# Two small softmax steps of the first two chunks on GpSimd instead of VectorE, in an attention + MoE + MoE kernel

## The chip, the cores and the metric

The kernel runs on one core of a Trainium2 chip. Its engines are TensorE (PE in the profile; PEld is its loading of weights), VectorE (DVE), ScalarE (ACT), GpSimd (POOL) and SyncE (SP, which here issues most DMAs). They run side by side and wait for each other through semaphores; each works through its own instructions in the order in which the program put them there. The metric is the device time of one execution in microseconds (us): lower is better. Before the change the median of 3 runs is 609.37 us (606.86 to 609.39).

## The reference

Three stages follow each other, on 4 batches x 576 positions = 2304 tokens of width 512:

```
scores = scale * q @ k^T, with block-causal mask (blocks of 64)      # 4 batches, 8 heads, 64 wide
scores = scores - max(scores);  attn = exp(scores)
attn   = attn / (sum(attn) + 1e-9);  x = attn @ v                    # -> x: 2304 x 512
h = max(x @ w1, x @ w2, x @ w3);  x = h @ w_out                      # first MoE, d_ff 768
skip_score = x @ w_skip; tokens with skip_score > 0 go to their best of 8 experts:
out = x + gate * relu(x @ w1[e]) @ w2[e];  the other tokens pass through
```

The softmax row steps of interest are the maximum, its scaling, the exponential with its sum, the addition of 1e-9, the reciprocal, and the multiplication by it.

## The kernel before

The tokens are cut into 6 chunks of 384. For each chunk the attention makes x (held as a high and a low part), and then the first MoE runs over the whole chunk. The attention of chunk c+1 is laid beside the MoE of chunk c, so that chunk 0's attention stands alone at the start and chunk 1's runs beside chunk 0's MoE. The second MoE follows at the end, from about 500 us on.

A unit of attention is one tile of up to 128 query rows, for one pair of heads. Chunk 0 has 12 units (3 tiles x 4 pairs), chunk 1 has 16 (per pair a tile over 512 keys, one of 64 rows over 576 keys, one of 64 rows over 64 keys, one over 192 keys). The 64-row tiles have both heads stacked, so their row statistics are one column; the others have two columns, one for each head. The steps of a unit, with the names by which rows show them:

- PE: scores `sc` (L611, and the mask L618), into one of 2 slots of PSUM
- DVE: negated row maxima `nm<-sc` (L628, L631; with two parts also L639), then the scaling of `nm` by 0.125 (L645)
- ACT: exponentials `p<-sc,nm` (L656), one for each head, which also leave the row sums in `su`; the score slot is free after these. Where the number of keys is no multiple of 128, GpSimd clears the tail of `p` (L653)
- DVE: `r<-su`, the sums plus 1e-9 (L667; with two parts L664), then the reciprocal (L671)
- ACT or DVE: `p` times `r` (L677 on ACT, L679 on DVE)
- PE: transposes `tp` (L691); ACT or DVE copies them to `pT` (L696); PE multiplies by v, `pv` (L710); ACT and DVE write the two parts of `x` (L720, L718)

In the first 122 us the weights of the first MoE also come in, as 64-bit words: 24 pieces (18 of w1, w2, w3, 6 of w_out), each decoded by ACT (L503, L528) and DVE (L511, L513, L515, L517, L532). A w_out piece also takes PE: four transposes `pswt` (L538) and four products `psw` (L547). The MoE of a chunk has 18 groups of 12 matmuls `ps_h` (L736), then six groups of 18 `ps_y` (L787), which need all 24 pieces in chunk 0.

The order on every engine comes from a planner that runs when the program is built (`Plan.order`). `build` gives it every step as a task: the engine (or a choice of engines), an assumed duration, a due time, the tasks that it depends on, and the buffers that it takes. The planner goes through the work once, takes on each engine the ready task with the earliest due time, and the program is written out in that order. Some durations and choices: a task that depends on one of another engine is taken as ready 0.13 to 0.20 us after that one's end; the multiplication by `r` may go to ACT or DVE, except in chunk 1, where it is ACT's; the copies of the transposes may go to DVE from chunk 2 on. A changed engine of one task thus changes the whole plan behind it.

The scaling and the addition are the tasks of L224 and L231; their instructions are in `s_max_scale` (L643) and `s_sum` (L659).

Of the kernel before, what the change touches and what calls it, by code (L numbers as in the profile page):

```python
# [13 lines left out]
ALU = mybir.AluOpType  # L14
# [3 lines left out]
B, H, S, D = 4, 8, 576, 64  # L18
# [138 lines left out]
def build(S, E, groups, units):  # L157
# [14 lines left out]
    for u in units:  # L172
        c = u[1]
# [9 lines left out]
    for i, (c, b, qlo, qhi, tiles, hp) in enumerate(groups):  # L183
        at = when[first_of[i]] - 12
# [10 lines left out]
    su = []  # L195
# [8 lines left out]
    for ks in su:  # L204
        at = when[ks[0]]
        dur, acq, deps = 0.0, [], [start]
        for k in ks:
            i, c, hp, q0, nq, nk, col, first = units[k]
            dur += nk * 4 / 2400 + 0.05
            acq += ["sc"] * (2 if nk > 512 and nq == P else 1)  # L210
            deps.append(kq[i])
        sc = S.add("PE", dur, at, lambda ks=ks: [E.sc(k) for k in ks], deps, acq, mode="R")
        tps = []
        for n, k in enumerate(ks):
            i, c, hp, q0, nq, nk, col, first = units[k]
            at = when[k]
            nkt = (nk + P - 1) // P
            sets, parts = (1, 2 if nk > 512 else 1) if nq == 64 else (2, 2 if nk > 512 else 1)
            w = nk // parts
            one = dve_time(w * 2 if sets == 2 else w * parts)  # L220
            mx = S.add("DVE", one * (parts if sets == 2 else 1), at - 2, lambda k=k: E.mx(k), [sc])
            if parts == 2:
                mx = S.add("DVE", 0.07, at - 2.5, lambda k=k: E.m2(k), [mx])
            mx = S.add("DVE", 0.07, at - 2.5, lambda k=k: E.ms(k), [mx])  # L224
            exs = []
            for j in range(sets):
                exs.append(S.add("ACT", parts * (0.24 + 0.83e-3 * w), at - 2 + 0.1 * j, lambda k=k, j=j: E.ex(k, j),
                                 [mx] + exs, ["p"] if j == 0 else []))
            for _ in range(2 if nk > 512 and nq == P else 1):
                later("sc", sc, *exs)  # L230
            rs = S.add("DVE", 0.07, at - 3, lambda k=k: E.ra(k), exs)  # L231
            rs = S.add("DVE", 0.08, at - 3, lambda k=k: E.rs(k), [rs])
            nms = []
            for j in range(sets):
                nm = S.add(dict(ACT=0.19 + 0.83e-3 * nk, **(dict(DVE=0.13 + 0.52e-3 * nk) if c != 1 else {})), 0, at - 2.5 + 0.1 * j, None, [rs])
                nm.emit = lambda k=k, j=j, nm=nm: E.nm(k, j, nm.on)
                nms.append(nm)
            todo = sets * nkt
            evs = []
            for m in range(0, todo, 4):  # L240
                z = min(4, todo - m)
                tp = S.add("PE", 0.107 * z, at - 1, lambda k=k, m=m: E.tp(k, m),
                           nms + [ident] + ([tp0] if m else []),
                           ["tp"] + (["pT"] if m == 0 else []), mode="T")
                ev = S.add(dict(ACT=act_time(128 * z), **(dict(DVE=dve_time(128 * z)) if c > 1 else {})), 0, at - 5, None, [tp])
                ev.emit = lambda k=k, m=m, ev=ev: E.ev(k, m, ev.on)
                later("tp", tp, ev)
                later("p", exs[0], tp)
                if m == 0:
                    tp0 = tp  # L250
                evs.append(ev)
            last_pv[k] = (tp0, evs, nkt)
        deps, dur, acq = [], 0.0, []
        for k in ks:
            i, c, hp, q0, nq, nk, col, first = units[k]
            deps += last_pv[k][1] + [vv[i]]
            dur += last_pv[k][2] * (0.213 if nq == P else 0.107)
            acq.append("tp")
        c = units[ks[0]][1]
        if c not in x_first:  # L260
            acq.append("x")
        pv = S.add("PE", dur, when[ks[0]] - 0.5, lambda ks=ks: [E.pv(k) for k in ks], deps, acq, mode="C")
        x_first.setdefault(c, pv)
        if pv is not x_first[c]:
            pv.deps.append(x_first[c])
        for k in ks:
            i, c, hp, q0, nq, nk, col, first = units[k]
            xh = S.add("ACT", act_time(nq), when[k] - 4, lambda k=k: E.xh(k), [pv])
            xl = S.add("DVE", dve_time(nq), when[k] - 4, lambda k=k: E.xl(k), [xh])
            later("tp", pv, xl)  # L270
            later("pT", last_pv[k][0], pv)
            all_x[c] += [xh, xl]
            sc_of.setdefault(units[k][0], []).append(sc)
            pv_of.setdefault(units[k][0], []).append(pv)
# [37 lines left out]
    for c in range(NCH):  # L312
# [3 lines left out]
        for f in range(NF):  # L316
            for i in range(3):
                at = base + (3 * f + i) * 2.1
# [126 lines left out]
def _moe1_phase(tc, nc, const, small, g):  # L445
# [12 lines left out]
    with ExitStack() as st_y:  # L458
# [183 lines left out]

        def s_max_scale(k):  # L643
            nm = ud[k]["nm"][:, 0:ud[k]["sets"]]
            nc.vector.tensor_scalar(nm, nm, 0.125, None, op0=ALU.mult)  # L645

        def s_exp(k, j):
            nk, u = units[k][5], ud[k]
# [10 lines left out]
        def s_sum(k):  # L659
# [4 lines left out]
                nc.vector.scalar_tensor_tensor(r[:, 0:sets], su[:, 0, 0:sets], 1e-9, su[:, 1, 0:sets],  # L664
                                               op0=ALU.add, op1=ALU.add)
            else:
                nc.vector.tensor_scalar(r[:, 0:sets], su[:, 0, 0:sets], 1e-9, None, op0=ALU.add)  # L667

        def s_recip(k):
            r = ud[k]["r"][:, 0:ud[k]["sets"]]  # L670
# [929 lines left out]
```

## Time and profile before

| what | us |
|---|---|
| median of 3 runs (lowest, highest) | 609.37 (606.86, 609.39) |
| the profiled execution | 609.76 |
| its span, first to last instruction | 607.1 |
| PE busy | 582.6 (96%) |
| DVE busy | 349.8 (58%) |
| ACT busy | 316.7 (52%) |
| POOL busy | 43.3 (7%) |

The span is what the trace shows; 2.66 us of the profiled execution lie outside it. Busy shares are means over stages that have different limits, so they are read by stretches: the stretches below were cut where PE first runs a matmul of the first MoE (41.33 us), where the last long run of `ps_h` of chunk 0 ends (94.1 us; the first piece of w_out is turned 0.9 us later), and where `ps_y` of chunk 0 starts (122.18 us). A row of a timeline has the start, the length, the engine, the source line, the operation with its tiles and shape, and in brackets the idle time of that engine before it and what ended that.

### The profile page before, as it was taken

The page shows a single profiled execution, that of the slowest core. Times are in us where ns is not written, and L with a number is a line of the kernel's source. Part 1 is how long each engine was busy: PE and PEld are TensorE (multiplying, and loading weights), DVE is VectorE, ACT ScalarE, POOL GpSimd, SP SyncE. Part 2 cuts the span into 40 slices and gives each one's busy share as a digit, 9 for nine tenths or more (in the row PEclk, how much of TensorE's full clock was granted, in tenths as well). Part 3 has the DMA queues.
Part 4 walks back from the last instruction along what each step waited for, and adds up shares of the span by engine and source line. Part 5 has one row for each costly group of instructions (what it writes and reads, how often), then busy time and mean ns, then how long its engine had stood idle before and what let it go on. Part 6 is the DMA issues. An engine that isn't in the chain of part 4 may idle for free. (4 is left out here: it accounts for less than half of the span.)

```text
span 607.1 us, 11847 instructions
## 1 busy us (share of the span) xinstructions
PE 582.6 (96%) x4338; PEld 495.5 (82%) x4338; DVE 349.8 (58%) x1022; ACT 316.7 (52%) x825; POOL 43.3 (7%) x101
## 2 busy tenths in 40 slices
PE   6889999899999999999999999999999999899994
PEld 3568798699888998988978889988899997688732
DVE  4899999925555346555366562565533675258600
ACT  4998869942757424545245444375641541158420
POOL 1000000002000010000200000200001011311101
PEclk9999999999999999999999999999999999899998
DMA  6564754421110220103211223100016752799980
GB/s 184 159 203 140 217 159 142 138 92 60 51 30 23 72 90 24 41 21 94 75 44 48 62 77 110 44 22 23 1 37 213 250 179 49 238 363 366 343 288 23
DMA packets 61096, 72.74 MB, mean 120 GB/s; under 512 B 7571, under 2 KB 40597, under 8 KB 61024
## 3 DMA queue, kind: packets, MB, share of 16 engines
q1 hardware_dynamic: 59424, 68.88, 35.5%
q0 software_dynamic: 1600, 2.96, 1.5%
q8 instruction: 39, 0.64, 0.5%
q14 instruction: 33, 0.27, 0.1%
HBM read 61.13 MB, written 11.04 MB: 119 GB/s over the span
## 5 line engine op out<-in xcount | busy, mean ns | idle before, releaser
L736 PE MATMUL ps_h<-x,w 128*128 128x384 f32 x1296 | 244.7, 341 | 0.5 <-DVE hm L745 0.5
L736 PEld LDWEIGHTS ps_h<-x,w 128*128 128x128 f32 x1296 | 222.4, 188 | 5.5 <-issue 3.3
L656 ACT ACTIVATE p<-sc,nm 128x288 f32<-128x288 f32 (+7 forms) x168 | 85.0, 516 | 29.6 <-DVE nm L645 28.9
L696 ACT COPY pT<-tp 128x512 f32<-128x512 f32 (+2 forms) x108 | 53.3, 511 | 47.9 <-PE tp L691 46.7
L611 PE MATMUL sc<-k,q 64*64 64x288 f32 (+9 forms) x384 | 67.8, 453 | 6.4 <-DMA q<-in_kq_dram 4.7
L691 PE MATMUL tp<-cst_sb,p 128*128 128x128 f32 x432 | 65.9, 281 | 3.9 <-ACT pT L696 1.8
L787 PE MATMUL ps_y<-wo,h_h 128*128 128x256 f32 (+1 forms) x360 | 68.8, 287 | 0.0
L691 PEld LDWEIGHTS tp<-cst_sb,p 128*128 128x128 f32 x432 | 49.7, 143 | 17.7 <-issue 8.0
L710 PE MATMUL pv<-pT,vt 128*64 128x128 f32 (+1 forms) x960 | 60.4, 270 | 1.6 <-ACT pT L696 1.5
L631 DVE TENSOR_REDUCE nm<-sc 128x2 f32<-128x256 f32 (+7 forms) x64 | 51.3, 811 | 15.8 <-PE sc L618 10.3
L710 PEld LDWEIGHTS pv<-pT,vt 128*64 128x64 f32 x960 | 48.0, 138 | 13.8 <-issue 4.9
L787 PEld LDWEIGHTS ps_y<-wo,h_h 128*128 128x128 f32 x360 | 56.7, 189 | 1.2 <-issue 1.2
L787 PE MATMUL ps_y<-wo,h_l 128*128 128x256 f32 (+1 forms) x180 | 51.1, 284 | 0.0
L611 PEld LDWEIGHTS sc<-k,q 64*128 64x128 f32 (+1 forms) x384 | 29.5, 178 | 24.2 <-issue 11.3
L677 ACT ACTIVATE p<-p,r 128x576 f32<-128x576 f32 (+8 forms) x73 | 42.3, 596 | 9.0 <-DVE r L671 8.3
L745 DVE TENSOR_TENSOR hm<-ps_h,ha 128x384 f32<-128x384 f32 x36 | 20.0, 555 | 34.6 <-PE ps_h L736 33.2
L720 ACT CAST x<-pv 128x128 fp32r<-128x128 f32 (+1 forms) x80 | 20.0, 263 | 31.2 <-PE pv L710 30.8
L656 ACT ACTIVATION_READ_ACCUMULATOR p<-sc,nm 128x1 f32 x168 | 35.0, 208 | 0.0
L745 DVE TENSOR_TENSOR hm<-ps_h,hm 128x384 f32<-128x384 f32 x36 | 20.0, 555 | 25.2 <-PE ps_h L736 24.6
L787 PEld LDWEIGHTS ps_y<-wo,h_l 128*128 128x128 f32 x180 | 34.0, 189 | 0.0
L718 DVE TENSOR_TENSOR x<-pv,x 128x128 fp32r<-128x128 f32 (+1 forms) x80 | 21.1, 274 | 21.6 <-ACT x L720 20.8
L749 ACT CAST h_h<-hm 128x384 fp32r<-128x384 f32 x36 | 18.5, 515 | 28.0 <-DVE hm L745 27.9
(220 smaller groups left out, 678.8 us busy)
## 6 DMA issues: line engine op xcount, KB each, us to landing
raw<-in_m_w_dram SPq DMA_DIRECT2D x19, 1024.0 KB, 7.2
raw<-in_w_dram SPq DMA_DIRECT2D x18, 512.0 KB, 3.8
vt<-in_v_dram SPq DMA_DIRECT2D x16, 320.0 KB, 3.3
x<-y SPq DMA_DIRECT2D x18, 256.0 KB, 2.1
out_dram<-y SPq DMA_DIRECT2D x18, 256.0 KB, 2.4
xa<-in_m_w_dram SPq DMA_DIRECT2D x4, 1024.0 KB, 6.8
xb<-in_m_w_dram SPq DMA_DIRECT2D x4, 1024.0 KB, 7.8
raw<-in_w_out_dram SPq DMA_DIRECT2D x6, 512.0 KB, 3.5
```

The costliest lines, as they stand in the source:

```text
L611: nc.tensor.matmul(bank[:, 0:hi - lo], gd["q"][rows, q0:q0 + nq], gd["k"][rows, lo:hi], start=True, stop=packed or hi != nk)
L631: nc.vector.tensor_reduce(nm, first_ps[:, :, 0:w], axis=AX.X, op=ALU.max, negate=True)
L656: nc.scalar.activation(u["p"][:, j, lo:hi], src, AF.Exp, bias=u["nm"][:, j:j + 1], scale=0.125, accum_out=u["su"][:, n, j:j + 1])
L677: nc.scalar.activation(pt, pt, AF.Copy, scale=r)
L691: nc.tensor.transpose(tp[:, n, :], u["p"][:, j, t * P:(t + 1) * P], ident)
L696: copy(u["pT"][:, m:m + z], u["tp", m][:, 0:z])
L710: nc.tensor.matmul(pv[64 * j:64 * j + 64, 0:nq], vt[:, t, 64 * j:64 * j + 64], pT, start=(t == 0), stop=(t == nkt - 1))
L718: nc.vector.tensor_tensor(xl, pv, xh, op=ALU.subtract)
L720: nc.scalar.copy(xh, pv)
L736: nc.tensor.matmul(ps, a[:, d, :], x[:, d, :], start=(n == 0), stop=(n == 3 * ND - 1))
L745: nc.vector.tensor_tensor(nxt, hm_at["ps", i], hm_at[f], op=ALU.max)
L787: nc.tensor.matmul(ps, a[:, f, hs], x[:, f, lo:hi], start=(n == 0), stop=(n == 3 * NF - 1))
```

## The change

In chunks 0 and 1 the scaling of the maxima, and the addition of 1e-9 where the row sums are in one part, are GpSimd's. The maxima, the exponentials, the reciprocals and the multiplications stay where they were. That is 28 scalings (12 in chunk 0, 16 in chunk 1; 20 of two columns, 8 of one) and 24 additions (all 28 units but the four over 576 keys).

```
--- before.py
+++ after.py
@@ -221,14 +221,14 @@
             mx = S.add("DVE", one * (parts if sets == 2 else 1), at - 2, lambda k=k: E.mx(k), [sc])
             if parts == 2:
                 mx = S.add("DVE", 0.07, at - 2.5, lambda k=k: E.m2(k), [mx])
-            mx = S.add("DVE", 0.07, at - 2.5, lambda k=k: E.ms(k), [mx])
+            mx = S.add("POOL" if c < 2 else "DVE", 0.07, at - 2.5, lambda k=k: E.ms(k), [mx])
...
-            rs = S.add("DVE", 0.07, at - 3, lambda k=k: E.ra(k), exs)
+            rs = S.add("POOL" if c < 2 and parts == 1 else "DVE", 0.07, at - 3, lambda k=k: E.ra(k), exs)
             rs = S.add("DVE", 0.08, at - 3, lambda k=k: E.rs(k), [rs])
...
         def s_max_scale(k):
             nm = ud[k]["nm"][:, 0:ud[k]["sets"]]
-            nc.vector.tensor_scalar(nm, nm, 0.125, None, op0=ALU.mult)
+            eng = nc.gpsimd if units[k][1] < 2 else nc.vector
+            eng.tensor_scalar(nm, nm, 0.125, None, op0=ALU.mult)
...
             else:
-                nc.vector.tensor_scalar(r[:, 0:sets], su[:, 0, 0:sets], 1e-9, None, op0=ALU.add)
+                eng = nc.gpsimd if units[k][1] < 2 else nc.vector
+                eng.tensor_scalar(r[:, 0:sets], su[:, 0, 0:sets], 1e-9, None, op0=ALU.add)
```

The source lines behind the change move by one or two (L667 of before is L669, L671 is L673, L691 is L693, L710 is L712, L736 is L738, L787 is L789).

On DVE, the first softmaxes of chunk 0 (`nm` maxima, `r` sums, `p` exponentials), before:

```order
L631 TENSOR_REDUCE nm<-sc 128x2
L645 TENSOR_SCALAR nm<-nm 128x2
L631 TENSOR_REDUCE nm<-sc 128x2
L645 TENSOR_SCALAR nm<-nm 128x2
L667 TENSOR_SCALAR r<-su 128x2
L671 RECIPROCAL r<-r 128x2
L679 TENSOR_SCALAR p<-p,r 128x128
L631 TENSOR_REDUCE nm<-sc 128x2
L667 TENSOR_SCALAR r<-su 128x2
```

and the same place on DVE in the changed kernel:

```order
L631 TENSOR_REDUCE nm<-sc 128x2 x2
L673 RECIPROCAL r<-r 128x2
L681 TENSOR_SCALAR p<-p,r 128x128
L631 TENSOR_REDUCE nm<-sc 128x2
L673 RECIPROCAL r<-r 128x2
L681 TENSOR_SCALAR p<-p,r 128x256
L631 TENSOR_REDUCE nm<-sc 128x2
```

The rows L645 and L667 are gone from here; the reciprocal now waits for GpSimd. Until the first `ps_h` product is read, two multiplications of `p` of 128x384 have also gone from DVE (6 before, 4 now) to ACT (2 before, 4 now).

The steps taken from DVE stand on GpSimd in the changed kernel like this, from behind the constants on (numbers are those of the buffers; before, GpSimd had nothing there up to the first clearing of `p`, in chunk 1):

```order
L646 TENSOR_SCALAR nm_184<-nm_184 128x2
L669 TENSOR_SCALAR r_199<-su_187 128x2
L669 TENSOR_SCALAR r_219<-su_192 128x2
L646 TENSOR_SCALAR nm_211<-nm_211 128x2
L646 TENSOR_SCALAR nm_235<-nm_235 128x2
L669 TENSOR_SCALAR r_269<-su_239 128x2
```

Scalings and additions of neighbouring units take turns in one queue, each behind the one in front of it.

On PE, a part of the stretch in which w_out is turned (`pswt`, `psw`) beside the last units of chunk 1, before:

```order
L710 MATMUL pv<-pT,vt 64x64 x10
L691 MATMUL tp<-cst_sb,p 128x128
L547 MATMUL psw<-wr_sb,wt 128x10 x4
L710 MATMUL pv<-pT,vt 64x64 x2
L691 MATMUL tp<-cst_sb,p 128x128 x4
L538 MATMUL pswt<-cst_sb,dec 128x128 x4
L611 MATMUL sc<-k,q 64x64 x2
L710 MATMUL pv<-pT,vt 64x128 x4
L547 MATMUL psw<-wr_sb,wt 128x10 x4
```

and on PE in the changed kernel, a part of the same stretch:

```order
L738 MATMUL ps_h<-x,w_121 128x384 x12
L538 MATMUL pswt<-cst_sb,dec 128x128 x4
L693 MATMUL tp<-cst_sb,p 128x128 x5
L611 MATMUL sc<-k,q 64x64 x2
L547 MATMUL psw<-wr_sb,wt 128x10 x4
L538 MATMUL pswt<-cst_sb,dec 128x128 x4
L712 MATMUL pv<-pT,vt 64x64 x2
L712 MATMUL pv<-pT,vt 64x128 x4
L738 MATMUL ps_h<-x,w_121 128x384 x12
L547 MATMUL psw<-wr_sb,wt 128x10 x4
```

Groups of `ps_h` now stand between the steps of w_out: behind the first `pswt` there are 3 of the 18, where before there was 1. In return the two pairs of scores of chunk 2 (over 320 and 448 keys), which stood in front of `ps_y` of chunk 0, stand behind it and one `ps_h` group. From the MoE of chunk 2 on, PE's order is the same in both kernels.

## Rows read from the trace of the kernel before

**Rows 1.** Stretches: length; busy us (x instructions) of each engine; granted clock, DMA share, GB/s

```profile
4.00:16.00 12.00, 10.45 (x52) 6.30 (x52) 6.95 (x26) 6.02 (x23) 0.00 (x0) 1.00 0.77 218
16.00:41.33 25.33, 20.78 (x186) 12.54 (x184) 23.95 (x77) 24.44 (x77) 0.15 (x1) 1.00 0.55 156
41.33:94.10 52.77, 52.77 (x393) 46.30 (x392) 52.16 (x126) 41.96 (x95) 0.61 (x4) 1.00 0.60 182
94.10:122.18 28.08, 25.77 (x252) 20.46 (x249) 25.69 (x87) 25.32 (x80) 1.93 (x9) 1.00 0.46 133
122.18:500.00 377.82, 377.32 (x2985) 342.58 (x2984) 193.83 (x595) 180.36 (x497) 22.60 (x52) 1.00 0.23 72
```

**Rows 2.** Waits of PE, 16 to 41.33 us: for what; us in total, times, longest

```profile
PE tp L691 <- ACT pT L696: 1.0, 2, 0.6
PE tp L691 <- DVE x L718: 1.0, 2, 0.5
PE sc L611 <- ACT p L656: 0.9, 2, 0.7
```

**Rows 3.** Waits of PE, 94.1 to 122.18 us

```profile
PE pv L710 <- ACT pT L696: 1.0, 2, 0.8
PE tp L691 <- ACT pT L696: 0.8, 1, 0.8
```

**Rows 4.** Timeline of DVE about the small steps, 42 to 43 us

```profile
42.38 0.16 DVE L667 TENSOR_SCALAR r<-su 128x2 f32<-128x2 f32 x1
42.45 0.15 DVE L639 TENSOR_TENSOR nm<-nm 128x1 f32<-128x1 f32 x1
...
42.98 0.15 DVE L645 TENSOR_SCALAR nm<-nm 128x1 f32<-128x1 f32 x1
43.09 0.43 DVE L513 TENSOR_SCALAR dec<-dec 128x512 int32<-128x512 int32 x1
```

**Rows 5.** The scaling (L645) until 122.18 us: its durations, who waited for it

```profile
L645 DVE TENSOR_SCALAR nm<-nm x30: 131/158/170, 6.8 to 121.2; 128x2 f32<-128x2 f32 x22, 128x1 f32<-128x1 f32 x8
...
  ACT p L656: 7.4, 6
```

**Rows 6.** Timeline: maxima of a unit on DVE, its first exponential on ACT, two units

```profile
6.35 0.42 DVE L631 TENSOR_REDUCE nm<-sc 128x2 f32<-128x256 f32 x1 [4.78 <-PE sc L618]
...
7.08 0.37 ACT L656 ACTIVATE p<-sc,nm 128x128 f32<-128x128 f32 x1 [4.83 <-DVE nm L645]
...
18.25 0.40 DVE L631 TENSOR_REDUCE nm<-sc 128x2 f32<-128x256 f32 x1
...
19.88 0.37 ACT L656 ACTIVATE p<-sc,nm 128x128 f32<-128x128 f32 x1
```

**Rows 7.** Groups until 122.18 us by shape: busy us, mean ns of one

```profile
L677 ACT ACTIVATE p<-p,r 128x384 f32<-128x384 f32 x2 | 1.2, 615 | 0.0
...
L515 DVE SCALAR_TENSOR_TENSOR dec<-raw,dec 128x512 int32<-128x512 int32 x24 | 16.5, 686 | 0.0
...
L511 DVE TENSOR_SCALAR dec<-dec 128x512 f32<-128x512 f32 x24 | 10.2, 424 | 0.7 <-ACT dec L503 0.6
```

**Rows 8.** Groups on POOL in the whole span, by shape

```profile
L653 POOL MEMSET p<- 128x64 f32 x16 | 2.5, 154 | 162.5 <-PE tp L691 88.8 <-DVE hm L745 48.6 <-ACT pT L696 11.8
...
L970 POOL IOTA eidx<- 128x8 f32 x1 | 0.1, 127 | 0.0
```

**Rows 9.** Timeline: a DVE step of the decoding and a clearing on POOL, 95.2 us

```profile
95.24 0.52 DVE L511 TENSOR_SCALAR dec<-dec 128x512 f32<-128x512 f32 x1
95.28 0.20 POOL L653 MEMSET p<- 128x128 f32 x1 [12.56 <-ACT dec L503]
```

**Rows 10.** Timeline: two groups of ps_h; scores of chunk 2, their first multiplication by r

```profile
41.33 4.45 PE L736 MATMUL ps_h<-x,w 128*128 128x384 f32 x24
...
117.52 0.81 PE L611 MATMUL sc<-k,q 64*128 64x320 f32 x4
...
123.85 0.39 DVE L679 TENSOR_SCALAR p<-p,r 128x320 f32<-128x320 f32 x1
```

## The prediction, as it stood before the changed kernel ran

> **What bounds the kernel now.** I first cut the span into stretches and read the busy time of each engine in them [rows 1]. From 122.18 to 500 us PE is idle for 0.5 of 377.8 us, with DVE and ACT about half idle: there PE is the bound, and nothing that DVE or ACT save can shorten it. The change is in the stretches before. From 4 to 16 us no engine is full. From 16 to 41.33 us, with chunk 0's attention and the first decoding, PE idles 4.55 us, DVE 1.4 and ACT only 0.9: ACT is the fullest engine, DVE close behind. From 41.33 to 94.10 us PE has no idle time at all, and DVE 0.6. From 94.10 to 122.18 us PE idles 2.3 us, DVE 2.4, ACT 2.8: each waits for the others.
>
> A gain must come out of PE's idle time up to 122.18 us: 1.55 + 4.55 + 0 + 2.31 = 8.4 us [rows 1], since PE's own work stays the same. Then I asked what these idle times wait for. From 16 to 41.33 us it is the copies of the transposes on ACT, the second part of x on DVE, and exponentials that hold the score slots, about 1 us each [rows 2]; later, 1.8 of 2.3 us are copies on ACT [rows 3]. So more of it is ACT's work than DVE's, although ACT's work is itself late when DVE is.
>
> Because PE is full behind 122.18 us, and its order is the same from the MoE of chunk 2 on, what is won or lost before it should reach the end whole.
>
> **The steps that go from DVE.** 28 scalings and 24 additions leave it. One takes 131 to 170 ns by its own record [rows 5], but DVE starts the next one sooner: the addition at 42.38 is followed at 42.45, the scaling at 42.98 at 43.09 [rows 4]. So a step occupies DVE for 0.07 to 0.11 us, 0.09 in the middle, and 52 of them for 4.7 us: 2.2 us for chunk 0's 24, 2.5 us for chunk 1's 28.
>
> **The steps that come to GpSimd.** It has 0.15 us of work up to 41.33 us and 2.5 us from there to 122.18 [rows 1], so it has room. How long a two-column step lasts there no row shows. The nearest are the iota of 128x8 (127 ns) and the clearing of 128x64 (154 ns), and the longer clearing of 128x128, 0.20 us [rows 8, 9]. I take 0.2 us, as the new step also reads, and bound it by 0.1 and 0.5. With a second hand-over between engines, I take 0.4 us from the end of the maxima to the exponential.
>
> Before, that way took 0.31 us when nothing lay between (maxima end at 6.77, exponential starts at 7.08) and 1.23 us for a usual unit (18.65 to 19.88) [rows 6]. In all of 30 units until 122.18 us ACT was idle only 6 times for the scaling, and 4.8 of those 7.4 us are the first unit of all [rows 5, 6]. So 0.4 us on GpSimd costs about 0.1 us on a handful of units and nothing on the others: ACT is busy with other work, or the scaling stood in DVE's queue behind decoding steps of 0.42 or 0.69 us [rows 7], which it now passes. I set hand-overs at zero, with +0.6 us as the bound (six units by 0.1). The cover is ACT's backlog; without it, the price is that of the last rival.
>
> The new waits: a reciprocal on DVE now waits for GpSimd, and behind it in DVE's queue stand maxima and decoding steps. Before, it waited for the addition in the same queue, which waited for the same exponentials. The difference is one hand-over, some 0.1 to 0.3 us of DVE for 24 units if DVE has no backlog, so at most what the change frees; in the stretches where DVE is full it is covered.
>
> **The order that comes with it.** Up to the first group of ps_h two multiplications of 128x384 go from DVE to ACT, 0.615 us each [rows 7], 1.2 us on the engine that has only 0.9 us idle from 16 us on. Up to 41.33 us the bounds are thus a gain of 2.2 us plus these two steps (at most 0.8 us on DVE, as no such step there is longer than the 424 ns of one over 512 columns [rows 7]) if DVE decides, so 3.0, and a loss of 1.2 us if ACT does. I take a gain of 0.5, a little below the middle (0.9), since ACT is the fuller engine [rows 1].
>
> From 41.33 to 122.18 us the limits are 0 and 2.31 us. DVE's freed 2.5 us are about PE's idle time, and three groups of ps_h instead of one now stand between the steps of w_out, where PE idled; a pair of groups is 4.45 us of PE work that waits for no copy of a transpose [rows 10]. I take 1.5 us.
>
> The two pairs of scores of chunk 2 move behind ps_y. Their PE time moves with them and costs nothing, but their softmax starts later. Before, from 117.52 us to the first multiplication at 123.85 was 6.3 us, hidden under ps_y [rows 10]. Now the cover behind them is two groups of ps_h, 4.45 us. The bounds are 0 and the 1.9 us between; DVE and ACT were delayed by the last units of chunk 1 at that time and are freer behind ps_y, so I take 0.2 us.
>
> Sum: 0.5 + 1.5 - 0.2 = 1.8 us off the profiled execution's 609.76, so 608.0. The median of the runs lies 0.4 us below that execution; I forecast 607.6 for the median.
>
> **Rivals.**
>
> *All that DVE gives is PE's.* DVE decides in both stretches: 2.2 + 2.3 = 4.5 us, so 604.9. For it: DVE is full from 41.33 to 94.10 and nearly so before [rows 1]. Against it: PE has no idle time in that same stretch, and the waits name ACT more often than DVE [rows 2, 3].
>
> *Nothing arrives.* ACT's extra 1.2 us eats what chunk 0 gives, and PE's idle time around w_out stays, since its waits are for ACT's copies [rows 3]: 609.4. For it: ACT's 0.9 us of slack from 16 us on.
>
> *Slower: VectorE and GpSimd hold each other up.* At 95.24 us a decoding step lasts 0.52 us instead of its mean of 0.42, and the one clearing that GpSimd has in that time starts within it [rows 7, 9]. If a GpSimd step that reads has to wait for the decoding step it meets, the 28 scalings come late. The decoding is 24 pieces of two steps of 0.42 and three of about 0.69, 2.9 us, or 70 us of the 106 us from 16 to 122 us. A scaling thus meets it two times in three; if it had to sit out the rest of a whole piece (1.45 us in the middle), it would be late by 0.95 us. Two score slots hide half; if half the units have spare time as that at 18.65 us has, 14 x 0.48 = 6.7 us are lost, less 1.8 won: about 614. It decides from a mean delay of 0.3 us on (14 x 0.15 = 2 us). Against it: the steps of a piece seldom stand in a row on DVE, others lie between, and the effect seen is 0.1 us.
>
> The Trainium skill has this as a rule (SBUF — State Buffer, "Who interferes with whom"): a VectorE step in a two-port mode, or with two SBUF inputs against a GpSimd step that reads, shares one port pair with GpSimd, and whoever starts first holds it to the end. By that rule all five decoding steps lock out the new GpSimd steps, and the result is this rival if the lock is taken again at once; the trace agrees as far as the 0.52 us go, but it has no GpSimd step here that reads.
>
> **How the numbers follow.** Forecast 607.6 (its own range 606.0 to 609.0): 0.48. All of it, 604.9: 0.18. Nothing, 609.4: 0.22. Slower, 614: 0.12. From the low case down to about 604.6 and from the slow one up to 612 the range leaves out 0.2. A change of 0.5% (3.0 us) is about what a measurement can tell from none: faster is below 606.3, slower above 612.4. Faster: 0.17 of the low case and a seventh of the forecast, 0.24. Slower: 0.1. The same: 0.66.
>
> **What the profile will show.** Right, if: PE's first ps_h starts between 40 and 42 us and ps_y of chunk 0 between 117 and 119 (some 1.6 us of that are only the moved scores); PE's idle time between them falls below 1.5 us; the steps on GpSimd last 0.1 to 0.3 us; ACT's waits for the scaling stay few. Wrong, if GpSimd's steps last 0.5 us or more, or ACT's waits for them grow beyond some 5 us without the first unit; if PE has new gaps of over 1 us behind ps_y; or if the stretch from the MoE of chunk 2 on changes its length by over 1 us, which would be a cause that is not in this sum.

## The result, and the profile after

The changed kernel takes 612.59 us in the median of 10 runs, the kernel before 609.37: a ratio of 1.0058, 95% interval 1.0042 to 1.0074. By that ratio it is slower by 3.5 us (3.2 us between the medians), where the prediction had it faster by 1.8. The profiled execution took 612.66 us, with a span of 610.8. Three executions in all, of 951 and 1132 us (the kernel before) and 1430 us (kernel 3 below), lie far from every other and are in no ratio and no mean.

Where the time went is read from a few moments that both kernels have, and from the fact that PE does the same products up to them.

| moment (us) | before | after | difference |
|---|---|---|---|
| first `ps_h` of chunk 0 | 41.33 | 43.48 | +2.15 |
| first `ps_y` of chunk 0 | 122.18 | 120.32 | -1.86 |
| first `ps_h` of chunk 2 | 220.40 | 224.09 | +3.69 |
| end of the span | 607.1 | 610.8 | +3.7 |

In this pair of profiles nothing is won or lost from the MoE of chunk 2 on: 386.7 us in both. (Over the profiles of all kernels below, this last part takes 384.3 to 388.0 us.) The stretches of the changed kernel, cut where [rows 1] are cut and once more at chunk 2 (length; busy us and instructions of PE, PEld, DVE, ACT, POOL; granted clock, DMA share, GB/s):

```profile
4.00:16.00 12.00, 9.99 (x50) 6.11 (x52) 4.65 (x14) 7.08 (x25) 1.74 (x8) 1.00 0.78 214
16.00:43.48 27.48, 22.39 (x189) 13.29 (x187) 23.25 (x61) 24.48 (x77) 5.79 (x18) 1.00 0.50 146
43.48:94.10 50.62, 50.05 (x396) 43.11 (x394) 49.55 (x114) 43.60 (x103) 6.52 (x18) 1.00 0.62 184
94.10:120.32 26.22, 25.49 (x224) 22.28 (x223) 23.82 (x66) 20.62 (x62) 5.27 (x20) 1.00 0.49 143
120.32:224.09 103.77, 103.15 (x833) 93.36 (x830) 48.49 (x143) 47.90 (x136) 5.92 (x16) 0.98 0.19 58
```

PE's idle time between `ps_h` and `ps_y` is 0.57 + 0.73 = 1.3 us where it was 2.31 [rows 1], so the part of the forecast that counted idle time came out by 1.0 of 1.5 us. But the granted clock of the last row is below 1, and it was 1.00 before. The same view over all the work up to chunk 2, and up to the first `ps_h`, of the kernel before:

```profile
0.00:220.40 220.40, 208.00 (x1681) 175.34 (x1682) 151.67 (x449) 147.44 (x407) 9.45 (x40) 1.00 0.40 118
4.00:41.33 37.33, 31.23 (x236) 18.85 (x236) 30.89 (x102) 30.46 (x99) 0.15 (x1) 1.00 0.62 176
```

and of the changed one:

```profile
0.00:224.09 224.09, 211.06 (x1681) 178.16 (x1682) 150.34 (x401) 145.17 (x403) 27.11 (x92) 0.99 0.39 116
4.00:43.48 39.48, 32.38 (x237) 19.40 (x237) 27.90 (x74) 31.57 (x102) 7.54 (x26) 1.00 0.59 167
```

The 3.69 us are 0.63 us more idle time (12.40 to 13.03) and 3.06 us that the same 1681 products last longer (208.00 to 211.06). Of these, 1.15 us lie before the first `ps_h` (31.23 to 32.38; the 237th product there is the `ps_h` at the edge). In both kernels PE's first products last nearly twice as long as the same ones later, and in the changed kernel this slow start lasts longer. Scores over 384 keys in the kernel before:

```profile
7.94 1.65 PE L611 MATMUL sc<-k,q 64*128 64x384 f32 x4 [0.57 <-ACT p L656]
...
16.09 0.92 PE L611 MATMUL sc<-k,q 64*128 64x384 f32 x4
```

and in the changed one, with the transposes behind them (six of them last 0.88 us later on):

```profile
15.57 1.63 PE L611 MATMUL sc<-k,q 64*128 64x384 f32 x4
17.18 1.31 PE L693 MATMUL tp<-cst_sb,p 128*128 128x128 f32 x6
...
25.02 0.92 PE L611 MATMUL sc<-k,q 64*128 64x384 f32 x4
```

These two rows alone are 1.14 us. The same scores take 1.63 us in the profiles of kernels 1, 3, 9 and 14 below too, which open in the changed kernel's order, and 1.65 in that of kernel 2, which has the order of before. The granted clock of these stretches is shown as 1.00 all the same. Another 1.7 us lie in one place, where `ps_y` of chunk 0 begins:

```profile
117.10:120.50 3.40, 3.39 (x31) 2.87 (x32) 2.75 (x9) 2.25 (x7) 0.38 (x2) 1.00 0.29 75
120.50:123.90 3.40, 3.40 (x17) 3.40 (x18) 0.64 (x4) 1.38 (x6) 0.23 (x1) 0.50 0.27 76
```

From 120.5 to 123.9 us PE ran at half its clock, 1.2 GHz in place of 2.4, and got through 17 products; in a kernel with the same order that kept its clock (the first experiment) it is 32 in the same stretch. Ahead of the fall stand the small products of the last two pieces of w_out (`psw`, 10 columns) and of chunk 1's last units.

The waits of PE from 16 us to the first `ps_h`, beside [rows 2], are of the same kinds; what stands out is the time that ACT's copies come late (us in total, times, longest):

```profile
PE pv L712 <- ACT pT L698: 1.9, 3, 1.0
PE tp L693 <- DVE p L681: 0.9, 1, 0.9
PE tp L693 <- ACT p L679: 0.7, 2, 0.4
```

From 94.1 us to `ps_y`, the 1.8 us of waits for copies [rows 3] are gone; these are left:

```profile
PE sc L611 <- ACT p L657: 0.6, 1, 0.6
PE pswt L538 <- DVE dec L517: 0.2, 1, 0.2
```

The scalings on GpSimd answer to [rows 5]:

```profile
L646 POOL TENSOR_SCALAR nm<-nm x28: 213/234/888, 6.8 to 119.8; 128x2 f32<-128x2 f32 x20, 128x1 f32<-128x1 f32 x8
...
who waited for it (us, times):
  ACT p L657: 10.1, 9
```

Their median is 0.234 us, near the 0.2 that was assumed, the longest 0.888. ACT waited 10.1 us, 9 times, where it was 7.4 us, 6 times. So the steps themselves look much as foreseen, and the question is what else changed.

### The profile page after: what moved, and what is told of

Read it like the earlier page. It is cut to its first block, busy times and chain, and to the rows that moved or that the text cites. A ratio compares the mean times of both kernels' runs of the same rounds, so it can differ in the third digit from the quotient of the medians.

```text
span 610.8 us, 11846 instructions
## 1 busy us (share of the span) xinstructions
PE 585.7 (96%) x4338; PEld 500.2 (82%) x4338; DVE 348.3 (57%) x974; ACT 314.6 (51%) x821; POOL 62.3 (10%) x153
## 5 line engine op out<-in xcount | busy, mean ns | idle before, releaser
L738 PE MATMUL ps_h<-x,w 128*128 128x384 f32 x1296 | 245.2, 341 | 0.5 <-DVE hm L747 0.5
L738 PEld LDWEIGHTS ps_h<-x,w 128*128 128x128 f32 x1296 | 222.2, 188 | 6.7 <-issue 4.0
L698 ACT COPY pT<-tp 128x512 f32<-128x512 f32 (+2 forms) x102 | 50.2, 509 | 47.9 <-PE tp L693 47.2
L789 PE MATMUL ps_y<-wo,h_h 128*128 128x256 f32 (+1 forms) x360 | 70.8, 292 | 0.0
L693 PE MATMUL tp<-cst_sb,p 128*128 128x128 f32 x432 | 65.7, 281 | 3.4 <-DVE p L681 0.9
L693 PEld LDWEIGHTS tp<-cst_sb,p 128*128 128x128 f32 x432 | 50.0, 143 | 16.8 <-issue 6.7
L712 PE MATMUL pv<-pT,vt 128*64 128x128 f32 (+1 forms) x960 | 60.0, 270 | 2.7 <-ACT pT L698 2.6
L712 PEld LDWEIGHTS pv<-pT,vt 128*64 128x64 f32 x960 | 47.9, 138 | 15.2 <-ACT pT L698 6.6
L789 PEld LDWEIGHTS ps_y<-wo,h_h 128*128 128x128 f32 x360 | 58.1, 193 | 1.3 <-issue 1.2
L789 PE MATMUL ps_y<-wo,h_l 128*128 128x256 f32 (+1 forms) x180 | 51.9, 288 | 0.0
L611 PEld LDWEIGHTS sc<-k,q 64*128 64x128 f32 (+1 forms) x384 | 29.9, 180 | 24.6 <-issue 10.2
L789 PEld LDWEIGHTS ps_y<-wo,h_l 128*128 128x128 f32 x180 | 34.7, 193 | 0.0
L796 ACT COPY y<-ps_y 128x256 f32<-128x256 f32 x30 | 11.2, 373 | 45.1 <-PE ps_y L789 45.0
```

The lines of the kernel that those rows point to most:

```text
L611: nc.tensor.matmul(bank[:, 0:hi - lo], gd["q"][rows, q0:q0 + nq], gd["k"][rows, lo:hi], start=True, stop=packed or hi != nk)
L693: nc.tensor.transpose(tp[:, n, :], u["p"][:, j, t * P:(t + 1) * P], ident)
L698: copy(u["pT"][:, m:m + z], u["tp", m][:, 0:z])
L712: nc.tensor.matmul(pv[64 * j:64 * j + 64, 0:nq], vt[:, t, 64 * j:64 * j + 64], pT, start=(t == 0), stop=(t == nkt - 1))
L738: nc.tensor.matmul(ps, a[:, d, :], x[:, d, :], start=(n == 0), stop=(n == 3 * ND - 1))
L789: nc.tensor.matmul(ps, a[:, f, hs], x[:, f, lo:hi], start=(n == 0), stop=(n == 3 * NF - 1))
```

## Experiments

Theory "order": the plan behind the changed engine puts the work of all engines into another order, and that order is worse. Rival "GpSimd": its steps are late or hold VectorE up. A third came up with the rows above, "clock": PE's clock falls to half, whatever brings it about. The table has every kernel that ran: its ratio to the kernel before on the same chip, the granted clock averaged over its runs (the kernel before has 0.995), and from the one profiled execution the first `ps_h`, the first `ps_h` of chunk 2, PE's idle time up to there, and the half clock before that.

| kernel | ratio (95%) | mean clock | ps_h 0 | ps_h 2 | idle | half clock |
|---|---|---|---|---|---|---|
| before | 1 | 0.995 | 41.33 | 220.40 | 12.40 | none |
| after | 1.0058 (1.0042 to 1.0074) | 0.990 | 43.48 | 224.09 | 13.03 | 3.4 us at 120.5 |
| 1 after's order, no GpSimd | 1.0040 (1.0023 to 1.0057) | 0.993 | 43.44 | 222.50 | 12.59 | none |
| 2 before's order, GpSimd | 0.9994 (0.9981 to 1.0007) | 0.994 | 42.21 | 221.20 | 12.12 | none |
| 3 chunk 0 alone | 1.0011 (0.9993 to 1.0030) | 0.994 | 41.92 | 224.06 | 12.40 | 3.4 us at 121.8 |
| 4 chunk 1 alone | 0.9927 (0.9910 to 0.9945) | 0.996 | 41.30 | 219.55 | 10.86 | none |
| 5 order of 4, no GpSimd | 1.0001 (0.9987 to 1.0016) | 0.995 | 41.46 | 220.55 | 12.01 | none |
| 6 before's order, no steps | 0.9983 (0.9967 to 0.9999) | 0.996 | 40.90 | 219.77 | 11.77 | none |
| 7 before, assumed 0.09 | 1.0091 (1.0059 to 1.0123) | 0.987 | 40.23 | 226.81 | 13.46 | 10.2 us at 115.8 |
| 8 after, early products | 1.0055 (1.0033 to 1.0076) | 0.991 | 43.83 | 222.92 | 10.43 | 3.4 us at 23.8 |
| 9 after, filled | 1.0062 (1.0042 to 1.0082) | 0.993 | 43.68 | 223.32 | 13.17 | none |
| 10 kernel 7, filled | 1.0087 (1.0065 to 1.0109) | 0.989 | 39.71 | 225.44 | 13.20 | 6.8 us at 118.0 |
| 11 after, assumed 0.35 | 1.0001 (0.9986 to 1.0015) | 0.995 | 39.84 | 220.39 | 13.08 | none |
| 12 kernel 4 again | 0.9971 (0.9957 to 0.9985) | 0.996 | 41.09 | 219.32 | 10.85 | none |
| 13 after, multiplications at home | 1.0017 (0.9999 to 1.0036) | 0.991 | 40.62 | 223.37 | 10.78 | 6.8 us at 118.1 |
| 14 after, assumed 0.20 | 0.9999 (0.9985 to 1.0013) | 0.994 | 44.29 | 224.79 | 12.61 | 6.8 us at 103.6 |
| 15 before, assumed 0.11 | 1.0016 (0.9997 to 1.0035) | 0.993 | 44.23 | 221.75 | 13.94 | none |

A profile is one execution of many: that of kernel 14 is the slowest of its 12 (614.16 us, median 609.46), those of kernels 2 and 4 are the slowest of their 12 and 6, those of kernels 5, 9 and 10 the fastest of their 12, 6 and 6, that of kernel 7 is close to its median.

The first `ps_h` does not have the same work ahead of it everywhere: 236 or 237 products in most kernels, 230 or 231 in kernels 3, 7, 10 and 11 (some 1.2 us less), 245 in kernel 14. And over the table it does not go with the ratio (correlation 0.08): kernels 14 and 15 have it latest and are level with the kernel before, kernel 7 has it early and is the slowest. The first `ps_h` of chunk 2 goes with the ratio (0.81).

### 1 and 2: the order without GpSimd, GpSimd without the order

Kernel 1 is the changed kernel with its plan as it is, but the steps executed by VectorE:

```
-            eng = nc.gpsimd if units[k][1] < 2 else nc.vector
-            eng.tensor_scalar(nm, nm, 0.125, None, op0=ALU.mult)
+            nc.vector.tensor_scalar(nm, nm, 0.125, None, op0=ALU.mult)
```

and likewise for the addition. Kernel 2 is the reverse: the kernel before with only these lines of the change, the planner still believing in VectorE.

> The order of the changed kernel on every engine, but the scalings and additions of chunks 0 and 1 are executed by VectorE again, at the places where the plan had them on GpSimd. Theory 'order' (the loss comes from the order that the planner made on a wrong idea of GpSimd's cost): as slow as the changed kernel or slower, 612 to 615 us, first ps_h group at 43 us or later. Theory 'engine' (GpSimd's steps themselves come late, through hand-overs and VectorE's decoding steps that lock them out): the loss is gone, 608 to 610 us, first ps_h group near 41.5 us.

> The order of the kernel before on every engine, but the 28 scalings and 24 additions are executed by GpSimd. Theory 'order': no loss, 607 to 609.5 us (VectorE is freed of some 4.7 us of work), first ps_h at 41.5 us or earlier. Theory 'engine': the loss is here, 611 to 614 us, first ps_h at 43 us.

Measured: 1.0040 for the order alone, 0.9994 for GpSimd alone. The order carries most of the loss with no step on GpSimd, and the very same steps cost nothing that the runs can tell in the order of before. Kernel 1's first `ps_h` is at 43.44, the changed kernel's at 43.48. (Kernel 2's profile has it 0.88 us late, all of it by the longer slow start: PE's products ahead of it take 32.33 us in place of 31.23.) Kernel 1's profile lost no clock at `ps_y`, the same stretch as above:

```profile
120.50:123.90 3.40, 3.40 (x32) 3.33 (x30) 0.88 (x6) 2.40 (x9) 0.00 (x0) 1.00 0.29 87
```

So with one order the clock fell in one kernel's profile and not in the other's. Kernel 1's runs have a mean clock of 0.993 against 0.990 for the changed kernel; whether GpSimd has a part in that is not shown: the two ratios, 1.0040 and 1.0058, have intervals that overlap.

### 3 and 4: one chunk at a time

The changed kernel with the condition `< 2` set to `== 0` (kernel 3) or `== 1` (kernel 4), in plan and instructions, planned anew.

> The change in chunk 0 alone (12 units), planned anew. If the loss is made in the stretch of chunk 0's attention (first ps_h 2.2 us late in the changed kernel), the whole loss or most of it is here: 611 to 613 us. If it is made beside the decoding of chunk 0's MoE, 609 to 610 us. Theory 'engine' has fewer locked-out steps here than in chunk 1 (9 of 24 GpSimd steps over 0.3 us), theory 'order' makes no statement on the sign but says that the first ps_h moves with the order.

> The change in chunk 1 alone (16 units), planned anew. If chunk 0's stretch makes the loss, this is at or below the kernel before: 606.5 to 609.5 us, as the stretch from 41 us to ps_y gained in the changed kernel. If steps locked out by VectorE's decoding make it, this is the slow half: 611 to 613 us.

Chunk 0 alone is level with the kernel before (1.0011), chunk 1 alone is faster than both (605.88 us, 0.9927). The two do not add up to 1.0058: each change of the engine plans everything behind it again.

### 5 and 12: is kernel 4's gain its order, GpSimd, or the chip?

Kernel 5 has kernel 4's order, but its steps on VectorE, by the edit of kernel 1. Kernel 12 is kernel 4 once more, on another chip.

> The order of the kernel that has the change in chunk 1 alone, but its scalings and additions executed by VectorE. If the 4 us that kernel won over the kernel before come from the order, this one wins most of them too: 605.5 to 607, with ps_y of chunk 0 starting near 120. If they come from VectorE's freed 2.5 us, this one loses them: 608.5 to 610.

> The change in chunk 1 alone once more, on the chip and beside the kernel before of this call: its 605.9 (0.993 of the kernel before) rest on 6 runs of one chip, and its order with the steps on VectorE ran at 1.000 on another. If the gain is the kernel's, 0.991 to 0.995; if it was the chip's, 0.998 to 1.001.

Kernel 5 came out at 1.0001, so the order alone gains nothing. Kernel 12 at 0.9971: the gain is there on a second chip, but less than half of it (607.48 us). PE's idle time up to chunk 2 shows the size: 12.01 us in kernel 5, 10.85 and 10.86 in kernels 12 and 4. So with chunk 1 alone the step that the prediction foresaw is real, 1.1 us in the profile. The runs' 0.3 to 0.7% are 1.8 to 4.4 us; no row shows where the rest of that comes from.

### 6: no steps at all

The order of before; the 52 steps do nothing in chunks 0 and 1, and the reciprocal reads the sums.

```
-            nc.vector.tensor_scalar(nm, nm, 0.125, None, op0=ALU.mult)
+            if units[k][1] >= 2:
+                nc.vector.tensor_scalar(nm, nm, 0.125, None, op0=ALU.mult)
...
```

> The order of the kernel before, with the 28 scalings and the 24 additions of chunks 0 and 1 left out altogether (the scaling of the maximum and the 1e-9 are missing from those two chunks). This takes the whole 4.7 us from VectorE with no GpSimd step and no hand-over. If VectorE's time is worth what the prediction's low rival said, 604.9; by the prediction's own two terms 607.6; if an order that stays as it was gives nothing back, 609 to 609.8.

0.9983, or 1.0 us (0.1 to 2.0 by the interval). That is all that VectorE's 4.7 us are worth in that order, with no hand-over to pay.

### 7 and 15: another order without any change of engine

```
-            mx = S.add("DVE", 0.07, at - 2.5, lambda k=k: E.ms(k), [mx])
+            mx = S.add("DVE", 0.09 if c < 2 else 0.07, at - 2.5, lambda k=k: E.ms(k), [mx])
```

Kernel 15 has 0.11 in its place.

> The kernel before with the duration that the planner assumes for the scalings of chunks 0 and 1 set to 0.09 us in place of 0.07, still on VectorE: no instruction changes, only the order from the end of chunk 0's attention on. If any other order of this stretch may move the time by some 3 us, it need not come out at the kernel before's 609.6: outside 608.6 to 610.6. If the loss of the changed kernel needs its own order or GpSimd, this one is within 1 us of the kernel before.

> The kernel before with 0.11 us in place of 0.07 as the assumed duration of the scalings on VectorE; 0.09 ran at 1.009 of the kernel before. If a larger number makes the plan worse step by step, it is at 1.009 or more. If the orders are draws around the kernel before, it may be anywhere from 0.993 to 1.010, with its half clock before 130 us and its first ps_h telling which.

An assumed duration that is changed by 20 ns makes the kernel 0.9% slower, no less than the whole change does; changed by 40 ns it is 0.16% slower, which the interval does not tell from nothing. So the loss does not grow with the number, and a loss of this size needs neither GpSimd nor the change. In kernel 7 it is the clock, in the stretch where w_out is turned:

```profile
112.40:115.80 3.40, 2.41 (x25) 1.61 (x24) 3.37 (x13) 2.84 (x11) 0.20 (x1) 1.00 0.46 131
115.80:119.20 3.40, 3.35 (x17) 2.57 (x16) 2.85 (x10) 1.16 (x5) 0.00 (x0) 0.50 0.03 6
119.20:122.60 3.40, 2.77 (x14) 2.77 (x14) 1.25 (x9) 2.38 (x9) 0.00 (x0) 0.50 0.31 89
122.60:126.00 3.40, 3.40 (x18) 3.40 (x17) 0.05 (x1) 1.45 (x4) 0.00 (x0) 0.50 0.00 0
126.00:129.40 3.40, 3.40 (x34) 3.20 (x33) 0.42 (x2) 0.75 (x3) 0.00 (x0) 0.99 0.29 87
```

PE had 1.0 us without work, the clock went to 0.50, and each stretch then held 14 to 18 products in place of 34. Half of 10.2 us is 5.1 us; the ratio stands for 5.5. (Up to chunk 2 this profile loses 6.4 us, 5.35 of them in longer products, and it gets 2.4 back behind it.)

### 8: products in front, against the slow start

PE's slow start lasts until about 16 us before and until about 18 us after (the rows over 384 keys in the section on the result).

```
+                if k == 0:
+                    for _ in range(20):
+                        nc.tensor.matmul(ps[0:64, 1, 384:512], mask_k, mask_q, start=True, stop=True)
```

> The changed kernel with 20 products of the two mask tiles (64 x 128, bf16) in front of PE's first scores, into a part of a score tile that nobody reads; PE waits for its first queries there until 4.0 us. If PE's slow first 18 us (a pair of 64x64 bf16 products at 0.26 us in place of 0.20) are part of the loss, the first ps_h starts near 42.3 in place of 43.5 and the time falls to about 611.3. If the order alone sets the first ps_h, it stays at 43.2 to 43.6, and the time at 612.2 to 612.9.

The ratio stayed at 1.0055, so nothing was won in the runs, and the first `ps_h` at 43.83. But this profile does not rule the slow start out. The early products did shorten it: the scores over 384 keys at 15.68 us took 1.54 us in place of 1.63, the six transposes behind them 0.88 in place of 1.31, and the next transposes start at 18.51 in place of 18.95. Then, at 23.8 us, the clock fell, as it did not in the changed kernel's profile:

```profile
20.40:23.80 3.40, 1.89 (x23) 1.22 (x18) 3.25 (x12) 3.40 (x11) 0.60 (x2) 1.00 0.20 59
23.80:27.20 3.40, 3.40 (x18) 1.82 (x15) 2.04 (x8) 2.46 (x10) 0.95 (x3) 0.50 0.32 107
```

and took the lead away. How much of the late first `ps_h` the slow start makes is left open by this run. (Its idle time in the table is less because the 20 products fill idle time at the start.)

### 9 and 10: products against the half clock

```
+            if k >= 22:
+                for _ in range(2):
+                    nc.tensor.matmul(ps.rearrange("p d c -> p (d c)")[:, 0:CH], w_piece(0, 0, 0)[:, 0, :], hid[0][:, 0, :], start=True, stop=True)
             for d in range(ND):
                 nc.tensor.transpose(ps[:, d, :], c[:, d * P:(d + 1) * P], ident)
```

> The changed kernel, with two more products of 128x384 (0.19 us each at full clock) in front of the transposes of each of the last two pieces of w_out, in PE's queue; nobody reads them. They add at most 0.8 us. If the loss is PE's clock, which fell to half at 120.5 us behind the small products of these pieces, it falls there less often: no half clock between 100 and 130 us, and the time between 611 and 611.9. If the order costs the time without the clock, the time goes up by 0.4 to 0.8 us: 613.0 to 613.4.

> The same filling (two products of 128x384 ahead of each of the last three pieces of w_out) in the kernel whose planner assumed 0.09 us for the scalings on VectorE, which ran at 613.5 with 10 us of half clock from 115.8 us on and PE idle 1.7 us before ps_y. Filling costs at most 1.1 us. If the half clock is the loss, 609 to 611. If not, 613.5 to 614.6.

Kernel 9's profile (the fastest of its 6 runs) has no half clock before 500 us, and PE's busy time up to chunk 2 is 0.9 us below the changed kernel's (211.06 to 210.15) although 0.8 us of products were added. But the runs give 1.0062, no gain. Kernel 10 still fell, 6.8 us in place of 10.2, and stayed at 1.0087. So filling moves the clock a little (0.990 to 0.993, 0.987 to 0.989) and does not pay. As a test of the clock it is inconclusive for kernel 9 and a miss for kernel 10, where the fall was not prevented.

### 11 and 14: the assumed duration of the GpSimd steps

```
-mx = S.add("POOL" if c < 2 else "DVE", 0.07, ...)
+mx = S.add("POOL" if c < 2 else "DVE", 0.35 if c < 2 else 0.07, ...)
```

and the same for the addition; 0.20 in kernel 14.

> The changed kernel with 0.35 us in place of 0.07 as the duration that the planner assumes for the steps on GpSimd, near what they lasted (0.33 to 0.38 in the mean). If the loss comes from a plan that prices these steps wrongly, it goes: 608.5 to 610. If any new order of this stretch draws its loss or gain anew, nothing ties it to either kernel: it may lie from 605 to 614, and its time goes with the half clock before 130 us and with the first ps_h.

> The changed kernel with 0.20 us in place of 0.07 as the assumed duration of the steps on GpSimd; 0.35 ran at 1.000 of the kernel before, 0.07 at 1.006. If what counts is how near the assumed duration is to the 0.33 to 0.38 that they lasted, it lies between: 609.5 to 612. If every new order draws its time anew, it may come out anywhere from 605 to 614, on either side of both.

Both are level with the kernel before: 1.0001 and 0.9999. The loss is gone with either number. With 0.35 the first `ps_h` starts at 39.84 us, and no clock was lost:

```profile
0.00:220.39 220.39, 207.31 (x1682) 175.49 (x1682) 147.93 (x398) 147.78 (x406) 30.70 (x92) 1.00 0.39 118
```

That fits a price that had been wrong, but 0.20 fits as well as 0.35, and its profile has the first `ps_h` later than any other (44.29, with 245 products ahead of it). I take it that two more orders were drawn and both were better, not that a right price gives a good order.

### 13: the multiplications back on their engines

In the changed kernel the planner may put each multiplication by `r` on ACT or DVE. Here chunk 0's are tied to the engines they had before:

```
...
+                if c == 0:
+                    home = "DVE" if (k, j) in ON_DVE else "ACT"
+                    both = {home: both[home]}
...
```

> The changed kernel, with each multiplication by r of chunk 0 tied to the engine that it had in the kernel before (14 on VectorE, 10 on ScalarE), so that none moves to ScalarE; the rest is planned anew. If the 2.15 us lost at the first ps_h are the multiplications that moved to ScalarE, it starts between 41 and 42 us, and the time falls to 609.5 to 611. If the rest of the new order loses them, it stays at 43 to 44 and the time at 612 to 613.

The first `ps_h` starts at 40.62 us, 2.9 us earlier, and the ratio falls from 1.0058 to 1.0017. So the plan in which the multiplications stay at home has no late first `ps_h`; but that plan differs in more than the multiplications. What happens to the first of them, one of 256 columns, is seen on ACT. First the changed kernel (start, length, operation; idle time before and what ended it, in brackets):

```profile
10.80 0.51 ACT L679 ACTIVATE p<-p,r 128x256 f32<-128x256 f32 x1
...
11.87 0.59 ACT L657 ACTIVATE p<-sc,nm 128x384 f32<-128x384 f32 x1
...
13.25 0.61 ACT L657 ACTIVATE p<-sc,nm 128x384 f32<-128x384 f32 x1
...
14.76 1.23 ACT L679 ACTIVATE p<-p,r 128x384 f32<-128x384 f32 x3
18.31 0.86 ACT L698 COPY pT<-tp 128x512 f32<-128x512 f32 x2 [2.32 <-PE tp L693]
```

then DVE beside it:

```profile
14.28 0.17 DVE L673 RECIPROCAL r<-r 128x2 f32<-128x2 f32 x1 [1.98 <-POOL r L669]
14.56 0.42 DVE L681 TENSOR_SCALAR p<-p,r 128x384 f32<-128x384 f32 x1
```

and kernel 13, the same unit on ACT, then on DVE:

```profile
11.09 0.58 ACT L664 ACTIVATE p<-sc,nm 128x384 f32<-128x384 f32 x1 [0.31 <-POOL nm L653]
...
11.99 0.59 ACT L664 ACTIVATE p<-sc,nm 128x384 f32<-128x384 f32 x1
...
16.09 0.58 ACT L705 COPY pT<-tp 128x512 f32<-128x512 f32 x1 [0.69 <-PE tp L700]
```

```profile
13.00 0.17 DVE L680 RECIPROCAL r<-r 128x2 f32<-128x2 f32 x1 [0.58 <-POOL r L676]
13.20 0.75 DVE L688 TENSOR_SCALAR p<-p,r 128x384 f32<-128x384 f32 x2
```

In the changed kernel the multiplication of 256 columns stands on ACT ahead of the exponentials of the next unit, which start at 11.87 in place of 11.09; then the exponentials of two units take turns, and the second one over these 384 keys starts at 13.25 in place of 11.99. The reciprocal is 1.28 us later, DVE stands idle for 1.98 us, its multiplication has its twin on ACT, in a group of three that ends at 15.99, and ACT then waits 2.32 us for PE. DVE's "<-POOL" names the last link of that chain: the addition of 0.2 us on GpSimd waited for the exponentials.

That the multiplications moved is not enough for the loss, though. Kernel 11 also has 4 of 384 columns on ACT, and one of 256 columns, at 11.34 us, ahead of the same exponentials. There the second exponential over 384 keys follows the first at 12.45, and PE reaches its fourth scores over 384 keys 2 us ahead of the changed kernel. The changed kernel:

```profile
32.23 0.92 PE L611 MATMUL sc<-k,q 64*128 64x384 f32 x4
```

and kernel 11:

```profile
30.19 0.92 PE L611 MATMUL sc<-k,q 64*128 64x384 f32 x4
```

Kernel 15, on the other hand, has every multiplication on the engine of before, and its first `ps_h` is at 44.23; it loses that behind 30 us, where PE waits for exponentials and copies on ACT. What the rows show, then, is what stands in ACT's queue and in which order. The changed kernel's order with only the engine of these multiplications swapped was not run.

Kernel 13 is not told from the kernel before by its ratio, and its profile reaches chunk 2 2.97 us later, though its PE idles less than any but kernel 8's (10.78 us up to there): its clock fell (0.991 in the mean), and the same 1681 products last 4.59 us longer than before:

```profile
0.00:223.37 223.37, 212.59 (x1681) 178.23 (x1682) 147.53 (x397) 147.71 (x407) 26.12 (x92) 0.98 0.38 117
```

### The clock over all kernels

Over the 16 changed kernels of the table the ratio goes with the mean clock: the correlation is -0.88, and 0.001 of clock (0.6 us of the span) goes with 0.9 us of time. The changed kernel has 0.9900, the kernel before 0.9946 in the runs beside kernel 1: of a span of 611 us that is 2.8 us, if PE is the bound all the time, where 3.5 were lost. This is a correlation: an order that idles PE can also be slow for other reasons, and the two kernels that were to break it (9 and 10) did not.

Two things on record speak against the clock as the whole cause. At the same granted clock the order of the changed kernel is still slower: the four runs of kernel 1 at 0.995 took 610.80 to 613.33 us, the three of the kernel before at 0.995 beside them 609.16 to 609.73, and the changed kernel's three best-clocked runs (0.993 to 0.995) 611.2 to 613.3. And the mean clock holds stretches that cost nothing or that both kernels have. The kernel before falls behind 500 us, which [rows 1] do not show, once among products and once at the end, where PE has none left:

```profile
523.90:527.30 3.40, 3.40 (x11) 2.66 (x10) 1.75 (x12) 0.60 (x1) 2.78 (x3) 0.58 0.43 94
602.10:605.50 3.40, 0.00 (x0) 0.00 (x0) 0.00 (x0) 0.00 (x0) 0.00 (x0) 0.63 0.04 6
```

## Why the prediction was wrong, step by step

- **What is right.** The GpSimd steps: 0.234 us in the median against 0.2 (0.33 to 0.38 in the mean, within the bound of 0.5), and they cost nothing that the runs can tell (kernel 2). The stretch from the MoE of chunk 2 on kept its length (386.7 us in both). The gain from 41.33 to 122.18 us was to be 1.5 us of PE's idle time, and 1.0 came, by the mechanism that was named: the waits for copies among the w_out steps are gone. The moved scores were to cost 0.2, with a bound of 1.9; they cost 0.62 us, when PE's transposes of that unit wait for a clearing on GpSimd.
- **The first step that failed** is "since PE's own work stays the same", the ground of the whole sum. PE does the same 1681 products up to chunk 2, but they last 3.06 of the 3.69 us longer: 1.15 us in the longer slow start, 1.7 us at half clock behind w_out. With it falls "what is won or lost before it should reach the end whole": the gain of 1.0 us in idle time did not. No term of the sum and no rival had the length of PE's products in it. [rows 1] show a granted clock of 1.00 in every stretch up to 500 us, the slow start among them.
- **The second** is "I take a gain of 0.5" up to the first `ps_h`, with bounds of +3.0 and -1.2. It was a loss of 2.15 us, 1.00 of it idle time of PE (6.10 to 7.10 us from 4 us on) and 1.15 the slow start. The bound counted the two multiplications that moved to ACT as ACT's work, 0.615 us each. The rows of kernel 13 show a loss through ACT's queue instead: a multiplication ahead of the next unit's exponentials, and exponentials of two units in turn, delay a chain of four engines. I had named the move and priced it by its duration, not by what stands behind it in ACT's queue. Which of the two in that queue makes the idle time is argued from the rows and was not tested apart.
- **Together**, PE's idle time up to chunk 2 was to fall by 0.5 + 1.5 - 0.2 = 1.8 us and grew by 1.00 - 1.0 + 0.62, or 0.63 as measured over the whole.
- **The rivals.** "Nothing arrives" (609.4) named ACT in the first stage, and was too small in size and wrong around w_out, where idle time did fall. The slower one, 614, was near in time and wrong in its mechanism. GpSimd does wait for decoding steps, as at 79.06 us:

```profile
79.00 0.68 DVE L515 SCALAR_TENSOR_TENSOR dec<-raw,dec 128x512 int32<-128x512 int32 x1
79.06 0.99 POOL L669 TENSOR_SCALAR r<-su 128x2 f32<-128x2 f32 x1 [5.42 <-ACT p L657]
79.59 0.42 DVE L511 TENSOR_SCALAR dec<-dec 128x512 f32<-128x512 f32 x1
```

  The addition lasts 0.99 us and ends with the second of the two DVE steps, which last 0.68 and 0.42 as ever. The rule that the prediction took from the Trainium skill (SBUF — State Buffer, "Who interferes with whom") agrees with that row, VectorE's step being the one in possession; but by kernel 2 the delay costs nothing that the runs can tell. The row that the prediction took for the rule, at 95.24 us [rows 9], does not show it: there VectorE's step began first and was the longer one for it (0.52 us), and the clearing that began second lasted its usual 0.20.
- **The signs that were named.** First `ps_h` (40 to 42) and first `ps_y` (117 to 119) failed at 43.48 and 120.32; PE's idle time between them, forecast below 1.5 us, is 1.3. ACT's waits grew to 10.1 us, 4.8 of them the first unit, which is past the 5 us that were to speak for GpSimd; but kernel 1 has 9.0 us without GpSimd, so most of the growth came with the order.
- **What stays open.** Why the slow start lasts longer and the clock falls more often in this order, and whether GpSimd has a part in it: kernel 1 and the changed one have the same order, and mean clocks of 0.993 and 0.990. And 0.2 of the 3.7 us are placed by no row.

The version that beats both is the change in chunk 1 alone: 605.88 us (0.9927, 0.9910 to 0.9945) on one chip and 607.48 (0.9971, 0.9957 to 0.9985) on another.

## What to carry to other kernels

Where a planner writes the order, an edit of one engine is an edit of the whole program: run the new order with the old engine, and the old order with the new engine, before the engine is given credit or blame, and nudge a number of the planner to see how far any new order moves the time (here from -0.7 to +0.9%). Price a step that moves to another queue also by what stands behind it there, not by its duration alone. And compare PE's busy time over the same products, not its idle time alone: a kernel can lose idle time and still be slower, when its clock falls.

## What the runs showed of the hardware

- PE's clock fell to half in stretches of small products and short gaps, and it need not look idle by its records first: in the changed kernel PE was busy for 3.39 of the 3.40 us ahead of the fall, in kernel 7 for 2.41, in kernel 8 for 1.89. It does not come in every execution of an order: the mean clock of the changed kernel's runs goes from 0.986 to 0.995.
- PE starts slowly, with a granted clock that reads 1.00: the scores over 384 keys took 1.63 to 1.65 us at 8 to 16 us and 0.92 later. Where the slow part ended differs between profiles, before 16.1 us in the kernel before and after 17.2 in the changed one.
- A GpSimd step of 128x1 or 128x2 lasts 0.21 to 0.23 us in the shorter half of the 52, about as long as the clearing of 128x128 (0.20) that has 64 times the elements and more; beside decoding steps it lasts up to 0.99 us.
